# Choosing matmul widths at run time: per expert on three engines, or per group of 12 or 24 products on TensorE alone

## The chip, the core and the metric

One core of one Trainium2 chip runs the whole program. The time is the device time of an execution in microseconds, from runs of the kernel on the chip: before the change a median of 905.44 us over 3 runs (902.94 to 908.5). TensorE (PE) multiplies; VectorE (DVE) and ScalarE (ACT) evict its results and convert; GpSimd (POOL) issues gathers and scatters by index; SyncE (SP) issues most other DMAs. SBUF is the on-chip memory, PSUM the banks that PE writes.

## What is computed

Linear attention with an exponential feature map, then a mixture of 8 experts in which each of 2304 tokens goes to one expert, then a dense block with a maximum over three products:

```python
x = num / den                                # attention, 4 x 8 heads x 576 tokens -> 2304 x 512
expert_idx = np.argmax(logits, axis=1)       # logits: cosine of x and 8 embeddings / tau
for e in range(8):
    mask = expert_idx == e
    h = np.maximum(x[mask] @ w1[e], 0.0)     # 512 -> 1024
    out[mask] = gate_w[mask, None] * (h @ w2[e])   # 1024 -> 512
h = np.maximum(np.maximum(x @ w1, x @ w2), x @ w3) # second block, 512 -> 768, float64 weights
y = h @ w_out                                # 768 -> 512
```

## The kernel before, in words

Every float32 operand of the experts and of the second block is split in two (H, rounded to fp32r, and L, the rest), and each product is three: wH x H, wL x H, wH x L. Weights come by DMA as `raw` tiles of 1 MB, ScalarE rounds them to `wH` and VectorE subtracts for `wL` (`split_w`, L893).

The attention ends near 204 us. The routing then holds, on the chip, how many tokens each expert has, and the list of tokens sorted by expert. GpSimd gathers rows of x in that order, 128 a tile (`gather`, L867); PE transposes a tile into PSUM (`turn`, L874) and ScalarE copies it to the long tile `xy`, whose columns are the sorted tokens.

How many columns an expert's products need is known only at run time. `Routing.sizes` holds 17 widths, 256 to 512 in steps of 16. For expert e, PE, ScalarE and VectorE load the index of the width (`regs`, L934), and `choose` (L967) builds a binary tree of `If`s with 17 leaves; each leaf is `arm` (L981), the whole expert written out at one width:

- 8 times `A` (L898): 12 products of 128 x N into one PSUM bank, ScalarE's relu and VectorE's subtraction into `hx`; `split_w` of the two second-layer tiles after f = 1 and 3; the turning of the tiles that the next expert needs after f >= 1;
- `split_x` (L888) for the next expert's tokens and `split_w` for its first-layer weights (for the last expert: `split_y(0)` and two conversions of second-block weights, `prep_m2`, L1077);
- 4 times `B` (L911): 24 products into one bank, ScalarE's copy to `xy`.

So a tree holds 17 x 192 products in PE's program, 192 of which run. After the eighth expert an `If` (L1235) passes over `redo`, which does experts of more than 512 tokens in pieces; it isn't taken here.

The second block (`second`, L1110) goes over token groups g of 512, 256, 512, 512 and 512 columns and six slices f of the hidden 768. `S1(g, f)` is 36 products in three banks: ScalarE copies the first bank to `m2m` (L1134), VectorE takes the maximum with the other two (L1136), ScalarE rounds (`hH`, L1138) and VectorE subtracts (`hL`). `S2(g, f)` multiplies that with `w_out`. The weights are float64: `prep_m2` makes float32 H and L of one half slice out of the two 32-bit halves, one operation of ScalarE (L1086), three of VectorE (L1087 to L1089), one of ScalarE (L1090) and one of VectorE (L1091). During g = 0 and 1 a conversion stands ahead of each S1:

```python
for f in range(NF):
    for g in (0, 1):
        n = 2 * f + 2 + g
        self.prep_m2(n)
        self.load_m2(n + 2)
        S1(g, f, (6, 7))
        if f:
            S2(1 - g, f - 1, ...)
```

All order is written by hand: each engine runs its instructions in program order and waits for semaphores.

Of the kernel before, what the change touches and what calls it, by code (L numbers as in the profile page):

```python
# [601 lines left out]
class Routing:  # L602


    STEP, MIN, CAP = 16, 256, 512

    def __init__(self, tc, gp, rp, NT, E):
        self.tc, self.nc, self.gp, self.rp = tc, tc.nc, gp, rp
        self.NT, self.E = NT, E
        self.sizes = list(range(self.MIN, self.CAP + 1, self.STEP))  # L610

    def prep(self, n):
# [28 lines left out]
        self.th = iota(rp, [1, len(self.sizes) - 1], [[self.STEP, len(self.sizes) - 1]], "th", base=self.MIN)  # L641
# [41 lines left out]
    def blocks(self, bank, wbank):  # L683
# [32 lines left out]
        nv = len(self.sizes) - 1  # L716
# [116 lines left out]
class Mlps:  # L833


    S = 256
# [27 lines left out]
    def row(self, nm, dt=F32):  # L864
        return self.pool.tile([128, 512], dt, tag="xs", name=nm, bufs=6)
# [8 lines left out]
    def turn(self, d):  # L874
        ps = self.bank()
# [22 lines left out]
    def A(self, N, f, slots=(0, 1)):  # L898
        nc, P = self.nc, 128
        xH, xL = self.xe  # L900
        ps = self.bank()
        for k in range(4):
            i = slots[k // 2]
            c = (k % 2) * 1024 + f * P
            for q, (w, x) in enumerate(((self.wH, xH), (self.wL, xH), (self.wH, xL))):
                nc.tensor.matmul(ps[:, 0:N], w[i][:, c:c + P], x[:, k, 0:N], start=(k == 0 and q == 0), stop=(k == 3 and q == 2))  # L906
        hH, hL = (h[f // 4][:, f % 4, 0:N] for h in self.hx)
        nc.scalar.activation(hH, ps[:, 0:N], AF.Relu)  # L908
        nc.vector.scalar_tensor_tensor(hL, ps[:, 0:N], 0.0, hH.bitcast(F32), op0=ALU.max, op1=ALU.subtract)  # L909

    def B(self, N, d, o, slots=(2, 3)):  # L911
# [3 lines left out]
        for f in range(8):  # L915
            i, c = slots[f // 4], (f % 4) * 512 + d * P
            for q, (w, h) in enumerate(((self.wH, hH), (self.wL, hH), (self.wH, hL))):
                nc.tensor.matmul(ps[:, 0:N], w[i][:, c:c + P], h[f // 4][:, f % 4, 0:N], start=(f == 0 and q == 0), stop=(f == 7 and q == 2))  # L918
        nc.scalar.copy(self.xy[:, d, bass.ds(o, N)], ps[:, 0:N])

    def experts(self, between):

        tc, nc, rt, ex, E, NT, S = self.tc, self.nc, self.rt, self.ex, self.E, self.NT, self.S
        ET = mybir.EngineType
        sizes = rt.sizes
# [7 lines left out]

        def regs(e):  # L934
# [142 lines left out]
    def prep_m2(self, n):  # L1077
        if n >= 12:
            return
# [188 lines left out]
```

## Time and profile before

| | us |
|---|---|
| median of 3 runs | 905.44 |
| the profiled execution, as timed | 905.33 |
| its span, first to last instruction | 903.6 |
| PE busy | 754.9 (84%) |
| VectorE busy | 392.5 (43%) |
| ScalarE busy | 336.2 (37%) |
| GpSimd busy | 139.9 (15%) |

The attention runs to about 204 us, the experts from 227 to 548, the second block from 560 to 888; the last scatters end the span. A row of the timeline gives the start, the duration, engine, line, operation and in brackets the idle time of the engine just before, with what ended it. Products are pipelined: a product's duration is longer than the distance to the next one. A branch isn't counted as busy; its records stand under the sequencer of an engine (PEldq is PE's).

### The profile page before, as it was taken

What the parts mean: (1) busy time and instruction counts of PE and PEld (TensorE: products, weight loads), DVE (VectorE), ACT (ScalarE), POOL (GpSimd) and SP (SyncE); (2) the same over time, 40 slices, a digit from 0 to 9 for tenths busy, and PEclk for the clock granted to TensorE, in tenths of its full rate; (3) what the DMA queues carried; (4) which work ended last, traced back from release to release, by engine and by line L of the source; (5) the groups of instructions that cost most, each with busy time, mean ns of one, the idle gap of its engine ahead of it and who ended that gap; (6) DMA issues with size and microseconds to landing.
All of it is one profiled execution on the core that took longest, in us unless ns stands there. A gap on an engine that the chain in (4) does not pass through costs nothing. (4 is left out here: it accounts for less than half of the span.)

```text
span 903.6 us, 13141 instructions
## 1 busy us (share of the span) xinstructions
PE 754.9 (84%) x5459; PEld 626.9 (69%) x5459; DVE 392.5 (43%) x591; ACT 336.2 (37%) x576; POOL 139.9 (15%) x111
## 2 busy tenths in 40 slices
PE   8899999991944998919596984788889999999993
PEld 6665666551944888919596984677778888888882
DVE  7966766773430524605151644655532212111210
ACT  4867576753521534605151542322212212112111
POOL 2733243405400100043000000000000201100001
PEclk9999999995886999959887996999899999999997
DMA  9715332246430425423222503332100100000001
GB/s 199 166 48 128 93 79 83 71 154 211 133 131 12 132 95 189 143 54 95 98 94 99 178 13 99 116 118 93 47 1 12 59 0 12 36 1 23 24 1 46
DMA packets 59795, 76.48 MB, mean 85 GB/s; under 512 B 11632, under 2 KB 41976, under 8 KB 59648
## 3 DMA queue, kind: packets, MB, share of 16 engines
q1 hardware_dynamic: 55712, 64.53, 23.6%
q0 software_dynamic: 3456, 9.46, 3.0%
q8 instruction: 83, 1.36, 0.7%
q14 instruction: 64, 0.52, 0.2%
q10 hardware_dynamic: 480, 0.61, 0.2%
HBM read 65.12 MB, written 9.46 MB: 83 GB/s over the span
## 5 line engine op out<-in xcount | busy, mean ns | idle before, releaser
L906 PE MATMUL b<-xeH,wH 128*128 128x256 f32 (+4 forms) x256 | 88.5, 346 | 69.9 <-issue 69.2
L1136 DVE TENSOR_TENSOR m2m<-m2m,b 128x512 f32<-128x512 f32 (+1 forms) x60 | 38.0, 634 | 164.5 <-PE b L1132 164.3
L906 PEld LDWEIGHTS b<-xeH,wH 128*128 128x128 f32 x256 | 54.4, 212 | 73.6 <-issue 71.1
L909 DVE SCALAR_TENSOR_TENSOR hxL<-b,hxH 128x256 fp32r<-128x256 f32 (+4 forms) x64 | 30.1, 492 | 165.5 <-ACT hxH L908 139.9
L1153 POOL DMA_INDIRECT out_dram<-raw,c2t x18 | 21.2, 1180 | 459.3 <-DVE m2h L1139 280.2
L906 PE MATMUL b<-xeH,wL 128*128 128x256 f32 (+4 forms) x256 | 86.0, 336 | 0.0
L906 PE MATMUL b<-xeL,wH 128*128 128x256 f32 (+4 forms) x256 | 85.6, 334 | 0.0
L341 POOL PARTITION_ALL_REDUCE mq<-pq x32 | 69.3, 2215 | 95.4 <-ACT pq L339 89.3
L896 DVE TENSOR_TENSOR wL<-raw,wH 128x2048 fp32r<-128x2048 f32 x32 | 72.6, 2289 | 18.1 <-ACT wH L895 16.8
L918 PE MATMUL b<-hxH,wH 128*128 128x256 f32 (+4 forms) x256 | 79.6, 311 | 0.0
L918 PE MATMUL b<-hxL,wH 128*128 128x256 f32 (+4 forms) x256 | 79.5, 311 | 0.0
L918 PE MATMUL b<-hxH,wL 128*128 128x256 f32 (+4 forms) x256 | 79.4, 310 | 0.0
L908 ACT ACTIVATE hxH<-b 128x256 fp32r<-128x256 f32 (+4 forms) x64 | 28.4, 447 | 136.8 <-PE b L906 112.3
L1138 ACT CAST m2h<-m2m 128x512 fp32r<-128x512 f32 (+1 forms) x30 | 17.4, 579 | 147.6 <-DVE m2m L1136 147.6
L1132 PE MATMUL b<-xeH,wH 128*128 128x512 f32 x144 | 57.5, 399 | 12.9 <-ACTq L1235 12.0
L895 ACT CAST wH<-raw 128x2048 fp32r<-128x2048 f32 x32 | 60.1, 1901 | 0.7 <-DVE bi L728 0.7
L1132 PE MATMUL b<-xeH,wL 128*128 128x512 f32 x144 | 57.0, 396 | 0.0
L1132 PE MATMUL b<-xeL,wH 128*128 128x512 f32 x144 | 56.9, 395 | 0.0
L906 PEld LDWEIGHTS b<-xeL,wH 128*128 128x128 f32 x256 | 54.2, 212 | 1.9 <-DVE xeL L886 0.2
L906 PEld LDWEIGHTS b<-xeH,wL 128*128 128x128 f32 x256 | 54.4, 212 | 1.4
L1149 PE MATMUL b<-wH,m2h 128*128 128x512 f32 x144 | 51.0, 414 | 0.0
L918 PEld LDWEIGHTS b<-hxH,wH 128*128 128x128 f32 x256 | 48.5, 189 | 1.4
(227 smaller groups left out, 1612.2 us busy)
## 6 DMA issues: line engine op xcount, KB each, us to landing
raw<-in_moe_w_dram SPq DMA_DIRECT2D x32, 1024.0 KB, 5.1
raw<-in_moe_w_dram SPq DMA_DIRECT2D x18, 512.0 KB, 3.7
q<-in_q_dram SPq DMA_DIRECT2D x8, 576.0 KB
kv<-in_v_dram SPq DMA_DIRECT2D x8, 512.0 KB, 6.6
x_d<-x SPq DMA_DIRECT2D x16, 256.0 KB, 2.1
kv<-in_k_dram SPq DMA_DIRECT2D x7, 512.0 KB, 6.1
raw<-in_moe_w_out_dram SPq DMA_DIRECT2D x6, 512.0 KB, 4.5
kv<-in_k_dram SPq DMA_DIRECT2D x2, 256.0 KB
```

The lines of the kernel that those rows point to most:

```text
L341: nc.gpsimd.partition_all_reduce(mx.rearrange("p a b -> p (a b)"), d.rearrange("p a b -> p (a b)"), P, ReduceOp.absmax)
L895: self.nc.scalar.copy(self.wH[i], r)
L896: self.nc.vector.tensor_tensor(self.wL[i], r, self.wH[i].bitcast(F32), op=ALU.subtract)
L906: nc.tensor.matmul(ps[:, 0:N], w[i][:, c:c + P], x[:, k, 0:N], start=(k == 0 and q == 0), stop=(k == 3 and q == 2))
L908: nc.scalar.activation(hH, ps[:, 0:N], AF.Relu)
L909: nc.vector.scalar_tensor_tensor(hL, ps[:, 0:N], 0.0, hH.bitcast(F32), op0=ALU.max, op1=ALU.subtract)
L918: nc.tensor.matmul(ps[:, 0:N], w[i][:, c:c + P], h[f // 4][:, f % 4, 0:N], start=(f == 0 and q == 0), stop=(f == 7 and q == 2))
L1132: nc.tensor.matmul(b, w[:, c], y[k], start=(k == 0 and q == 0), stop=(k == 3 and q == 2))
L1136: nc.vector.tensor_tensor(m, m, b, op=ALU.max)
L1138: nc.scalar.copy(hH, m)
L1149: nc.tensor.matmul(ps[banks[c]], h[:, cs], w, start=(f == 0 and q == 0), stop=(f == NF - 1 and q == 2))
L1153: nc.gpsimd.indirect_dma_start(out=self.out, out_offset=bass.IndirectOffsetOnAxis(ap=rt.c2t[:, t:t + 1], axis=0), in_=o, in_offset=None)
```

## The change

Four widths (256, 320, 448, 512) take the place of 17. The index is loaded on PE alone, except for the very first group. Each A and each B builds its own tree of four bodies on PE (`pick`); the evictions stand behind the tree, once, on all 512 columns. 16 products on whole banks come first, on PE. Gathers are issued tile by tile as their four buffers (six before) come free, and the loads of the next weights stand right behind the split that frees a tile. The last expert does three conversions of second-block weights instead of two. In the second block a conversion is taken apart: `rebias` (ScalarE) for the next piece and `cut` (VectorE, three operations in one buffer, two buffers by turns) for this piece stand ahead of the products of S1, `high` and `low` behind its maxima; S2 of the last slice stands ahead of S1.

```diff
-    STEP, MIN, CAP = 16, 256, 512
+    WIDTHS, CAP = (256, 320, 448, 512), 512
...
-    S = 256
+    S = 512
...
-        return self.pool.tile([128, 512], dt, tag="xs", name=nm, bufs=6)
+        return self.pool.tile([128, 512], dt, tag="xs", name=nm, bufs=4)
...
+    def pick(self, idx, unit, lo=0, hi=None):
+        W = self.rt.WIDTHS
+        hi = len(W) if hi is None else hi
+        if hi - lo == 1:
+            return unit(W[lo])
+        m = (lo + hi) // 2
+        with self.tc.If(idx < m) as c:
+            self.pick(idx, unit, lo, m)
+        with c.Else():
+            self.pick(idx, unit, m, hi)
...
+        self.pick(idx, unit) if idx is not None else unit(512)
+        hH, hL = (h[f // 4][:, f % 4] for h in self.hx)
+        nc.scalar.activation(hH, ps, AF.Relu)
+        nc.vector.scalar_tensor_tensor(hL, ps, 0.0, hH.bitcast(F32), op0=ALU.max, op1=ALU.subtract)
...
+        nxt, idx0 = regs(0), index(0, ET.PE, ET.Activation, ET.DVE)
+        for i in range(16):
+            nc.tensor.matmul(self.ps[i % 8], self.wH[0][:, 0:128], self.wH[0][:, 0:512], start=True, stop=True)
...
+            for f in range(8):
+                if f == 1 and e == 0:
+                    for t in todo:
+                        self.gather(t)
+                self.A(idx0 if first else idx, f, first=first)
+                first = []
+                if f in (1, 3):
+                    self.split_w(2 + f // 2)
+                    if e + 1 < E:
+                        ex.load(2 + f // 2, e + 1)
+                if f >= 4 and todo:
+                    t = todo.pop(0)
+                    keep(t, self.turn(self.xs.pop(t)))
+                    if t + 4 < NT:
+                        self.gather(t + 4)
+            if e + 1 < E:
+                self.split_x(self.xy[:, :, bass.ds(nxt[1] + S, 512)])
+                for i in range(2):
+                    self.split_w(i)
+                    if e + 2 < E:
+                        ex.load(i, e + 2)
+                    else:
+                        self.load_m2(i)
             else:
...
+                self.split_y(0)
+                self.m2_job(3)
             between(e)
...
+            for d in range(4):
+                self.B(idx, d, off)
...
+        def cut():
+            V.tensor_scalar(t, t, 3, None, op0=ALU.logical_shift_left)
+            V.scalar_tensor_tensor(t, lo, 29, t, op0=ALU.logical_shift_right, op1=ALU.bitwise_or)
+            V.scalar_tensor_tensor(t, hi, -0x80000000, t, op0=ALU.bitwise_and, op1=ALU.bitwise_or)
+            self.load_m2(n + 2)
...
+            now, then = prep
+            if then:
+                then[0]()
+            if now:
+                now[1]()
             for i in range(3):
...
+            hH, hL = hT(g, f)
+            if now:
+                now[2]()
             nc.scalar.copy(hH, m)
+            if now:
+                now[3]()
             nc.vector.tensor_tensor(hL, m, hH.bitcast(F32), op=ALU.subtract)
...
         for f in range(NF):
             for g in (0, 1):
...
+                if f:
+                    S2(g, f - 1, b2[g])
+                S1(g, f, (6, 7), (parts.get(n), parts.get(n + 1)))
+                n += 1
```

On PE, where one A of an expert ends and the next begins, before the change (`b` is the PSUM bank, `xeH` and `xeL` the tokens, `wH` and `wL` the weights):

```order
L906 MATMUL b_2878<-xeL,wH_2860 128x256
L906 MATMUL b_2878<-xeH,wH_2860 128x256
L906 MATMUL b_2878<-xeH,wL_2864 128x256
L906 MATMUL b_2878<-xeL,wH_2860 128x256
L906 MATMUL b_2879<-xeH,wH_2859 128x256
L906 MATMUL b_2879<-xeH,wL_2863 128x256
L906 MATMUL b_2879<-xeL,wH_2859 128x256
```

And after the change, the end of the fourth body of one A and the beginning of the next A's tree:

```order
L923 MATMUL b_2881<-xeH,wH_2862 128x512
L923 MATMUL b_2881<-xeH,wL_2866 128x512
L923 MATMUL b_2881<-xeL,wH_2862 128x512
L905 UNCONDITIONAL_BRANCH
L905 COMPARE_AND_BRANCH x2
L923 MATMUL b_2882<-xeH,wH_2861 128x256
L923 MATMUL b_2882<-xeH,wL_2865 128x256
L923 MATMUL b_2882<-xeL,wH_2861 128x256
```

Between two banks stand now a branch and two compares, and three bodies that aren't run. PE's whole program has 10979 rows instead of 30813.

On ScalarE, the beginning of the second block before the change (`raw` under L1086 is the conversion's buffer, `m2m` the running maximum, `m2h` its rounded copy, `y1H` the second group's tokens):

```order
L1105 CAST y1H_38355<-xy 128x512
L1105 CAST y1H_38357<-xy 128x512
L1086 ACTIVATE raw_2509<-raw_2276 128x1024
L1090 CAST wH_2860<-raw_2509 128x1024
L1134 COPY m2m<-b_2880 128x512
L1138 CAST m2h<-m2m 128x512
L1086 ACTIVATE raw_2509<-raw_2505 128x1024
L1090 CAST wH_2860<-raw_2509 128x1024
L1134 COPY m2m<-b_2881 128x256
```

And after it (the running maximum is a part of `xy` now):

```order
L1129 CAST y1H_13298<-xy 128x512
L1093 ACTIVATE raw_2511<-raw_2507 128x1024
L1093 ACTIVATE raw_2511<-raw_2278 128x1024
L1167 COPY xy<-b_2882 128x512
L1102 CAST wH_2862<-raw_2511 128x1024
L1173 CAST m2h<-xy 128x512
L1093 ACTIVATE raw_2511<-raw_2507 128x1024
L1167 COPY xy<-b_2883 128x256
L1102 CAST wH_2863<-raw_2511 128x1024
```

The copy of the first bank has moved ahead of the rounding of the weights (L1090, now L1102), which waits for three operations of VectorE.

On ScalarE, the end of the last expert, before:

```order
L1105 CAST xeH<-xy 128x2048
L1086 ACTIVATE raw_2509<-raw_2276 128x1024
L1090 CAST wH_2859<-raw_2509 128x1024
L1086 ACTIVATE raw_2509<-raw_2505 128x1024
L1090 CAST wH_2859<-raw_2509 128x1024
L919 ISA
L919 COPY xy<-b_2880 128x256
```

and after:

```order
L1093 ACTIVATE raw_2511<-raw_2278 128x1024
L905 UNCONDITIONAL_BRANCH x4
L1102 CAST wH_2861<-raw_2511 128x1024
L1093 ACTIVATE raw_2511<-raw_2507 128x1024
L1102 CAST wH_2861<-raw_2511 128x1024
L1093 ACTIVATE raw_2511<-raw_2278 128x1024
L1102 CAST wH_2862<-raw_2511 128x1024
L945 ISA
L945 COPY xy<-b_2882 128x512
```

A third conversion stands ahead of the evictions of the last B (L919, now L945).

## Rows read from the trace of the kernel before

**Rows 1.** The page: the span, and part 1, busy time of PE.
```profile
span 903.6 us, 13141 instructions
...
PE 754.9 (84%) x5459; PEld 626.9 (69%) x5459; DVE 392.5 (43%) x591; ACT 336.2 (37%) x576; POOL 139.9 (15%) x111
```
**Rows 2.** Waits of PE, 205 to 575 us: total, times, longest.
```profile
PE b L906 <- issue: 69.2, 7, 23.6
PE b L1132 <- ACTq L1235: 12.0, 1, 12.0
```
**Rows 3.** Line L975, branches on PE's sequencer, ns min/median/max; stretches: engines' busy us, clock, DMA.
```profile
L975 PEldq COMPARE_BRANCH  x4: 65/65/78, 329.6 to 330.0; - x4
...
L975 PEldq COMPARE_BRANCH  x1: 3567/3567/3567, 325.5 to 325.5; - x1
...
L975 PEldq COMPARE_BRANCH  x1: 4869/4869/4869, 352.9 to 352.9; - x1
...
L975 PEldq COMPARE_BRANCH  x1: 6723/6723/6723, 515.6 to 515.6; - x1
...
325.53:329.10 3.57, 3.57 (x18) 3.00 (x17) 0.00 (x0) 0.00 (x0) 0.00 (x0) 1.00 0.02 5
352.86:357.73 4.87, 2.30 (x20) 2.10 (x18) 0.29 (x1) 0.37 (x1) 0.00 (x0) 1.00 0.93 363
```
**Rows 4.** Stretches, three of eight experts: busy us, clock, DMA share, GB/s.
```profile
227.00:259.00 32.00, 31.63 (x212) 31.16 (x212) 17.96 (x26) 16.90 (x25) 9.22 (x6) 0.91 0.51 177
...
330.00:358.50 28.50, 25.02 (x208) 24.82 (x208) 14.83 (x15) 15.38 (x22) 0.00 (x0) 1.00 0.43 149
...
523.00:548.00 25.00, 24.70 (x192) 24.50 (x192) 15.42 (x17) 11.40 (x14) 0.00 (x0) 0.93 0.14 44
```
**Rows 5.** Second block: waits of PE, 560 to 700 us; the stretch to 668.
```profile
PE b L1132 <- ACT m2m L1134: 16.6, 6, 4.2
...
580.50:668.00 87.50, 75.14 (x360) 64.17 (x360) 48.68 (x58) 24.57 (x33) 0.00 (x0) 0.90 0.22 72
```
**Rows 6.** Straight code, 664 to 867 us: the stretch; PE's instruction queue (packets, MB, share).
```profile
664.00:867.00 203.00, 203.00 (x898) 166.50 (x898) 43.99 (x59) 35.88 (x55) 17.35 (x14) 0.99 0.05 19
...
q8 instruction: 8, 0.13, 0.3%
```
**Rows 7.** Timeline of PE, 32 products apart; one S1 on the chain that ended last.
```profile
241.01 0.30 PE L906 MATMUL b<-xeH,wH 128*128 128x304 f32 x1
...
245.42 0.30 PE L906 MATMUL b<-xeL,wH 128*128 128x304 f32 x1
...
685.00 8.19 PE b L1132 x36
```
**Rows 8.** Start of the experts: third gather, landing of gathers, first product.
```profile
211.09 1.89 POOL L871 DMA_INDIRECT xs<-x_d,s2t  x1 [0.30 <-issue]
...
DMA to landing us min/median/max: 6.3/6.9/7.5
...
227.32 0.62 PE L906 MATMUL b<-xeH,wH 128*128 128x304 f32 x1 [0.68 <-ACT xeH L885]
```
**Rows 9.** Timeline of ScalarE around the joint to the second block.
```profile
544.16 1.05 ACT L1090 CAST wH<-raw 128x1024 fp32r<-128x1024 f32 x1 [4.44 <-DVE raw L1089]
...
549.82 1.04 ACT L1090 CAST wH<-raw 128x1024 fp32r<-128x1024 f32 x1 [3.55 <-DVE raw L1089]
...
560.40 1.14 ACT L1105 CAST y1H<-xy 128x512 fp32r<-128x512 f32 x2 [8.45 <-ACTq L1235]
...
566.85 0.58 ACT L1134 COPY m2m<-b 128x512 f32<-128x512 f32 x1
```
**Rows 10.** Timeline of PE at a short wait; the stretch around it.
```profile
587.23 0.50 PE L1132 MATMUL b<-xeH,wH 128*128 128x512 f32 x1 [0.91 <-ACT m2m L1134]
...
583.00:597.00 14.00, 10.56 (x57) 8.73 (x55) 8.90 (x10) 4.24 (x6) 0.00 (x0) 1.00 0.29 93
```

More of the change, by code (lines that the diff above doesn't have):

```diff
@@ new lines, in experts, with bring @@
+            todo = [t for t in range(4 * (e + 1), 4 * (e + 2)) if t < NT]
+            first = []
+            if e == 0:
+                for t in (2, 3):
+                    def bring(t=t, ps=self.bank(), d=self.xs.pop(t)):
+                        v = self.turn(d, ps)
+                        self.direct(v, t)
+                        keep(t, v)
+                    first.append((t, bring))
+            for f in range(8):
+                if f == 1 and e == 0:
+                    for t in todo:
+                        self.gather(t)
+                self.A(idx0 if first else idx, f, first=first)
+                first = []
+                if f in (1, 3):
[7 more added lines that the diff above has]
+                        self.gather(t + 4)
@@ L1045, in redo @@
             for d in range(4):
-                self.B(512, d, at)
+                self.B(None, d, at)
         self.split_y(0)
@@ L1085, in prep_m2, with rebias, high, low @@
         H, L = self.WH[f][:, o], self.WL[f][:, o]
[L1086 to L1091 removed]
+        V = nc.vector
+        def rebias():
+            nc.scalar.activation(t.bitcast(F32), hi.bitcast(F32), AF.Copy, scale=REBIAS)
+        def cut():
[3 more added lines that the diff above has]
+            self.load_m2(n + 2)
+        def high():
+            nc.scalar.copy(H, t.bitcast(F32))
+        def low():
+            V.tensor_tensor(L, t.bitcast(F32), H.bitcast(F32), op=ALU.subtract)
+        return rebias, cut, high, low
+    def m2_job(self, k):
+        for _ in range(k):
+            if self.m2n < 12:
+                for p in self.m2_parts(self.m2n):
+                    p()
+                self.m2n += 1
     def split_y(self, g):
@@ L1116, in second, with hT, S1 @@
         hq = self.ew.tile([P, 4, 512], F32R, tag="q", name="m2h", bufs=2)
-        hs = self.row("m2h1", F32R)
-        mm = self.row("m2m")
-        hT = {512: [(hq[:, 2 * i], hq[:, 2 * i + 1]) for i in range(2)], 256: [(hs[:, 0:256], hs[:, 256:512])] * 2}
-        def S1(g, f, banks, prep=None):
+        mm = self.xy[:, 0, self.S + self.NTOK:]
+        def hT(g, f):
+            if g == 1:
+                return hq[:, 2, 0:256], hq[:, 2, 256:512]
+            i = 2 * (f % 2) if g else 0
+            return hq[:, i], hq[:, i + 1]
+        def S1(g, f, banks, prep=(None, None)):
             H, L = self.ys[g]
```

169 lines of the change are left out of this document (49 added, 120 removed).

## The prediction

> **What bounds the kernel now.** I read the page first: the span, and TensorE (PE) busy 84% of it [rows 1]. The question is then what the other 16% are, so the waits of PE come next, for the expert stage alone: 69.2 us before the first product of an expert (L906), in 7 pieces, with "issue" as the releaser, and 12.0 us before the second stage, released by ScalarE's sequencer at the `If` of L1235 [rows 2]. "Issue" means that PE waited for no semaphore that the profile shows. The records of the branch instructions on PE's sequencer say what it did. Four in a row that were not taken stand at 329.6 to 330.0, 65 to 78 ns each and about 0.12 us apart; a branch out of an arm over one further arm took 3.6 us, one over sixteen arms 4.9 us, and one from the third arm to the end of its tree 6.7 us [rows 3]. So a taken branch to a far place costs 3.6 us or more, while PE's instruction queue reads, and one that falls through costs a tenth of a microsecond.
>
> Two more things stand in these rows. While the 4.9 us branch ran, 20 matmuls still started: the sequencer is some 17 to 20 products ahead of PE, about 2 us at 256 columns. And length goes with traffic: 3.6 us at a DMA share of 0.02, 4.9 us at 0.93 [rows 3].
>
> The second cost of a wait is the clock. Each expert stretch shows a granted clock of 0.90 to 0.95 (two of seven shown), the one that starts without a long wait 1.00 [rows 4]: after a far branch PE runs some microseconds at the lower level. Length times (1 - clock) is 32 x 0.09 = 2.9 us in the first and 25 x 0.07 = 1.8 us in the last, 16.6 us over all seven.
>
> The second stage has its own waits: 16.6 us in 6 pieces for ScalarE's first copy of `m2m` (L1134) [rows 5], and a clock of 0.90 over the 87.5 us from 580.5 to 668 [rows 5], thus 8.7 us. After 668 PE never waits: 203.0 us busy of 203 [rows 6].
>
> **The change part by part.** The sum goes against the profiled execution: span 903.6 us [rows 1], 905.33 us as timed, beside a median of 905.44 us. The inputs give 291, 494, 122, 198, 430, 296, 283 and 190 tokens per expert: before 304, 496, 256, 256, 432, 304, 288, 256 columns, after 320, 512, 256, 256, 448, 320, 320, 256.
>
> (a) Far branches between experts go. The trees of 17 arms of 192 products are replaced by trees of four bodies of 12 or 24. No branch then passes more than three bodies. The 69.2 us go, and the 16.6 us of low clock with them: -85.8.
>
> (b) Wider products: 96 columns more over the eight experts, 192 products each. 304 columns come every 0.138 us ((245.42 - 241.01)/32), 512 every 0.227 us (8.19/36) [rows 7], so 0.00043 us per column: 96 x 192 x 0.00043 = +7.9.
>
> (c) Branches inside the experts: 96 groups, each with two compares and one branch out. Not taken, 0.12 us each. A taken branch within a loaded stretch is not in this trace: from below 0.065 us, the shortest record, from above 3.6 to 6.7 us, the far ones. I take 0.2 us, next to the short ones, because target and branch stand at most three bodies apart, and keep the upper end as a rival. At 0.2 us a group costs the sequencer 0.5 us; the 17 products that it is ahead (2 us) cover that. +0.
>
> (d) Reading the code. On the straight stretch from 664 to 867 PE's instruction queue read 8 blocks (0.13 MB, 16 KB each), seven intervals, over 898 products [rows 6]: a block holds 128 products. Now three of four bodies are read and not run. A group of 12 holds 48 products, so a block lasts 128/48 = 2.7 groups, each 12 x 0.117 = 1.4 us at 256 columns (0.138 less 48 x 0.00043): 3.7 us, against 15 us of straight code; 4.6 us at 320 columns, 6.5 at 448 and 7.3 at 512. If the next block is requested when the last is entered, its time must stay below that. The nearest rows are the far branches: 3.6 us with DMA idle, 4.9 to 6.7 us with DMA busy [rows 3]. The weights of an expert keep the DMA share at 0.43 in a 256-column one [rows 4], so a good part of the reads meets traffic. The bounds are 0 (every block in time) and 90 us: 768 products per expert are 6 blocks, 36 in the six experts of 256 or 320 columns, each late by 6.7 - 4.2 = 2.5 us on average. I take +24: half of the 36 late by 1.3 us, since the queued products cover some and idle DMA the rest. The Trainium skill ("Runtime: NRT & Kernel Launch", Instruction fetch mechanics) says that code is read sequentially in 16 KiB blocks, that crossing a block is mostly hidden, and that a branch stalls when its target lies outside the two loaded blocks. The 16 KB and the stalls agree with rows 3 and 6; by its "mostly hidden" this term would be 0 and the sum 24 us lower, by the busy rows it is not.
>
> (e) The start. Tile 2 was ready long before PE came back from two far branches: its gather was issued at 211.09 and such a gather lands 6.9 us later, at 218.0, but the first product stood at 227.32 [rows 8]. Now turn and cast of tile 2 follow the landing, about 1.6 us: first product at 219.6, -7.7. The 16 warm-up products lie in the wait for tiles 0 and 1.
>
> (f) ScalarE and VectorE work on 512 columns always. In a 256-column expert they are busy 15.4 and 14.8 us of 28.5 [rows 4]; 12 evictions of twice the width would have to take over a microsecond more each to reach PE. Their 96 branches, one a group, lead to the next instruction of their own. Gathers now have four buffers instead of six, but each is issued a whole expert ahead, so PE is not late for them. +0; were a tile late, its 6.9 us would show once per expert.
>
> (g) The joint to the second stage. Three conversions instead of two now stand ahead of the last expert's evictions on ScalarE. One takes 549.82 - 544.16 = 5.66 us [rows 9]; so the evictions start 5.7 us later after the last A than before. What goes is one of the two far branches that ScalarE took in the 8.45 us before 560.40, about 4.2 us, and some 3 us of the 6.45 us from there to the first copy of `m2m` at 566.85 [rows 9], which no longer waits for a conversion. The copy thus comes about 1.5 us earlier, some 29 us after the last A, and PE's 12.0 us wait does not vanish: it moves into the first three groups of the second stage, which need that copy to free a bank. Of the next wait, of 4.2 us [rows 5], the pipelined order saves a part: together -4. If the joint gains nothing it costs those 4 us.
>
> (h) The second stage proper. `rebias` of the next piece and `cut` of this one are issued before the products, `high` and `low` behind the copy of `m2m`. That copy no longer stands behind a whole conversion of 5.66 us. From 580.5 to 668 VectorE is busy 48.7 us and PE 75.1 of 87.5 [rows 5], so the conversions fit beside the products once nothing waits for them in turn, and S2 ahead of S1 gives the chain more cover. The other five waits go (16.6 - 4.2 = 12.4), with 8.7 us of low clock: -21.1.
>
> Sum: -85.8 + 7.9 + 24 - 7.7 - 4 - 21.1 = -86.7. From 903.6 that is a span of 816.9; with the 1.7 us around it 818.6, about **819 us**.
>
> **The rivals.**
> 1. Code reading decides: at every block DMA is busy, so (d) reaches its upper end, 90 us. For it: the 4.9 us branch ran under traffic, and the 6.7 us one is longer still, and loads now follow each other sooner. Against: idle gaps remain. 819 + 66 = 885 us, still faster.
> 2. Near branches cost a read like far ones (slower). Each group has one branch out, and the eight experts take 0, 1, 1 or 2 inward (72 in all): 168 taken branches. At 3.6 us, the least of rows 3, these are 605 us of the sequencer's time, of which its 2 us of lead hide at most 192 over 96 groups: 413 us more than without (d), 795 + 413 = some 1210 us. It turns the sign from 1.15 us per group uncovered (110 us over 96). For it: no short taken branch is on record, and even the one over a single arm took 3.6 us. Against: what a far branch waits for is a block that isn't there, and straight code shows no wait at its block borders [rows 6], so the next block is there when it is reached.
> 3. The clock drops from many small gaps (slower too): at the lower of its two levels, half the other, the experts' 240 us of products grow by some 190 us (not all of a product's spacing is the clock's; an estimate): about 1000 us. Rows speak against it: a gap of 0.91 us at 587.23 left the clock at 1.00 [rows 10]. The Trainium skill ("TensorE: Matmul & The Clock Gate", A second HAM failure mode) describes such a kernel, in which short idles between groups of matmuls throttled the clock again and again; the trace has no such case.
> 4. The second stage keeps its waits, because the conversion's loads or VectorE end last: 21 us less gain, 840 us.
>
> **How the numbers follow.** Forecast 0.62, rival 1 0.17, rival 4 0.08, rival 2 0.06, rival 3 0.04, and 0.03 for a mixture that ends within 1% of 905. About 1% is what a measurement of this kernel can tell from no change (its runs spread 0.6%). Faster: 0.62 + 0.17 + 0.08 = 0.87; same 0.03; slower 0.10. The range goes from 790 (nothing late in (d), a little more at the joint) to 880, most of rival 1; what is left out is rivals 2 and 3 and the end of 1.
>
> **What would show it.** Right: no wait of over 2 us before A or B in the waits of PE; branch records of 0.1 to 0.3 us, some of 1 to 3 us at 256 and 320 columns, none at 512; clock 1.00 in the experts; no wait for `m2m` after the first f; instruction blocks at 16 KB, about 50 in the experts. Wrong: branch records of 3 us in every group (rival 2), spacings of 0.25 us (rival 3), waits in the 512-column expert as well (rival 1), or a joint longer than 45 us from the last A to the end of the second group.

## The result and the profile after

The changed kernel takes 806.69 us, the median of 4 runs (804.78 to 813.77); the kernel before took 904.95 us on the same chip (4 runs, 902.94 to 908.5). The ratio is 0.8925, with a 95% interval from 0.8862 to 0.8987. The forecast was 819 us in a range from 790 to 880. The profiled execution of the changed kernel is the longest of the four, 813.77 us; that matters below.

The page of the kernel after, its span and part 1, against [rows 1]. PE runs the same products, a little wider, and 16 more at the start. Its busy time falls by 4.1 us only, the span by 92.1 us: what went is mostly waiting (148.7 us in which PE wasn't busy before, 60.7 us after).

```profile
span 811.5 us, 13326 instructions
...
PE 750.8 (93%) x5475; PEld 620.5 (76%) x5475; DVE 403.0 (50%) x591; ACT 351.8 (43%) x576; POOL 140.5 (17%) x113
```

Waits of PE in the kernel after, 205 to 575 us (total, times, longest), against [rows 2]:

```profile
PE b L1165 <- ACTq L1269: 13.0, 1, 13.0
PE b L923 <- issue: 5.0, 2, 2.7
...
PE b L942 <- issue: 0.8, 3, 0.4
```

The 69.2 us of "issue" ahead of the first A have become 5.8 us, in five pieces ahead of A and B. The wait at the `If` in front of the second stage is still there, 13.0 us instead of 12.0.

Branch records of the kernel after, ns min/median/max, 205 to 480 us, against [rows 3]:

```profile
L905 PEldq COMPARE_BRANCH  x276: 65/176/4341, 219.4 to 476.2; - x138
```

By the trace's records 120 of the 276 last at most 0.09 us (branches not taken), 121 last 0.1 to 0.3 us, 24 last 0.3 to 1 us and 11 longer; the branches between arms took 3.6 to 6.7 us. The longest, 4.34 us, begins at 326.1, inside an expert of 256 columns.

Stretches of the kernel after (busy us of PE, PEld, DVE, ACT, POOL, then clock, DMA share, GB/s), against [rows 4] for the third and fourth expert (256 columns both) and [rows 5] for 87.5 us of the second stage from its third S1 on.

```profile
300.60:325.30 24.70, 24.70 (x209) 24.70 (x208) 16.77 (x15) 17.49 (x22) 3.01 (x2) 1.00 0.44 148
325.40:354.50 29.10, 26.22 (x201) 25.44 (x201) 17.29 (x16) 16.98 (x20) 0.00 (x0) 0.94 0.46 159
...
512.00:599.50 87.50, 87.50 (x469) 75.48 (x468) 48.04 (x61) 27.54 (x39) 1.99 (x2) 1.00 0.21 73
```

Read the third and fourth experts together: same width, same work, 24.70 us at clock 1.00 and 29.10 us at 0.94. The difference is mostly one late block of code. The trace keeps the start and the duration of every packet of PE's instruction queue, 16 KB each: one ran from 328.07 to 329.06 us, and the branch that began at 326.10 ended at 330.44, 1.38 us after it. All 11 records of over 1 us end 1.4 to 1.5 us after such a packet has landed. The second stage's beginning, which had 75.1 us of PE in 87.5 us at clock 0.90, is now without a gap at 1.00.

Where the time went is read from five points of PE's timeline. Of the kernel before (start, duration, engine, line): the first gather of the stage (POOL), the last product of the experts, the first product behind the first two S1 (it belongs to the third S1), the last product.

```profile
206.57 1.30 POOL L871 DMA_INDIRECT xs<-x_d,s2t  x1 [27.48 <-issue]
...
547.70 0.28 PE L918 MATMUL b<-hxL,wH 128*128 128x256 f32 x1
...
580.23 0.63 PE L1132 MATMUL b<-xeH,wH 128*128 128x512 f32 x1
...
887.52 0.39 PE L1149 MATMUL b<-hxH,m2h 128*128 128x512 f32 x1
```

And of the kernel after, with the first product of the experts, which before stood at 227.32 [rows 8]. The first product behind the first two S1 belongs to an S2 here (L1186), since S2 now stands ahead of the third S1:

```profile
209.99 1.30 POOL L872 DMA_INDIRECT xs<-x_d,s2t  x1 [27.33 <-issue]
...
223.06 0.64 PE L923 MATMUL b<-xeH,wH 128*128 128x320 f32 x1 [0.67 <-ACT xeH L886]
...
478.26 0.28 PE L942 MATMUL b<-hxL,wH 128*128 128x256 f32 x1
...
509.11 0.39 PE L1186 MATMUL b<-wH,m2h 128*128 128x512 f32 x1
...
795.40 0.39 PE L1186 MATMUL b<-hxH,m2h 128*128 128x512 f32 x1
```

| stretch | before | after | difference | predicted |
|---|---|---|---|---|
| up to the first gather (not changed) | 206.57 | 209.99 | +3.4 | 0 |
| to the first product of A | 20.75 | 13.07 | -7.7 | -7.7 |
| experts | 320.38 | 255.20 | -65.2 | -53.9 |
| to the end of the first two S1 | 32.53 | 30.85 | -1.7 | -4 |
| second stage from there | 307.29 | 286.29 | -21.0 | -21.1 |
| tail | 16.1 | 16.1 | 0 | 0 |
| span | 903.6 | 811.5 | -92.1 | -86.7 |

### The profile page after: what moved, and what is told of

It reads as the page before. It is cut to its first block, busy times and chain, and to the rows that moved or that the text cites. A ratio compares the mean times of both kernels' runs of the same rounds, so it can differ in the third digit from the quotient of the medians.

```text
span 811.5 us, 13326 instructions
## 1 busy us (share of the span) xinstructions
PE 750.8 (93%) x5475; PEld 620.5 (76%) x5475; DVE 403.0 (50%) x591; ACT 351.8 (43%) x576; POOL 140.5 (17%) x113
## 5 line engine op out<-in xcount | busy, mean ns | idle before, releaser
L1169 DVE TENSOR_TENSOR xy<-xy,b 128x512 f32<-128x512 f32 (+1 forms) x60 | 38.0, 634 | 173.9 <-PE b L1165 173.4
L923 PE MATMUL b<-xeH,wH 128*128 128x320 f32 (+3 forms) x256 | 84.4, 330 | 3.3 <-issue 2.4
L931 DVE SCALAR_TENSOR_TENSOR hxL<-b,hxH 128x512 fp32r<-128x512 f32 x64 | 42.7, 687 | 87.6 <-ACT hxH L930 85.7
L923 PE MATMUL b<-xeL,wH 128*128 128x320 f32 (+3 forms) x256 | 83.0, 324 | 2.7 <-issue 2.7
L923 PE MATMUL b<-xeH,wL 128*128 128x320 f32 (+3 forms) x256 | 82.9, 324 | 0.0
L942 PE MATMUL b<-hxH,wH 128*128 128x320 f32 (+3 forms) x256 | 81.6, 319 | 0.9 <-issue 0.8
L942 PE MATMUL b<-hxL,wH 128*128 128x320 f32 (+3 forms) x256 | 81.0, 316 | 0.0
L942 PE MATMUL b<-hxH,wL 128*128 128x320 f32 (+3 forms) x256 | 81.0, 316 | 0.0
L1165 PE MATMUL b<-xeH,wH 128*128 128x512 f32 x144 | 57.6, 400 | 13.0 <-ACTq L1269 13.0
L930 ACT ACTIVATE hxH<-b 128x512 fp32r<-128x512 f32 x64 | 38.2, 600 | 58.1 <-PE b L923 57.8
L896 ACT CAST wH<-raw 128x2048 fp32r<-128x2048 f32 x32 | 60.0, 1901 | 0.6 <-DVE bi L729 0.6
L1165 PE MATMUL b<-xeL,wH 128*128 128x512 f32 x144 | 57.5, 399 | 0.7 <-DVEq L1269 0.7
L1165 PE MATMUL b<-xeH,wL 128*128 128x512 f32 x144 | 57.2, 397 | 0.0
L942 PEld LDWEIGHTS b<-hxH,wL 128*128 128x128 f32 x256 | 48.5, 189 | 1.7
```

The source lines that it names most:

```text
L896: self.nc.scalar.copy(self.wH[i], r)
L930: nc.scalar.activation(hH, ps, AF.Relu)
L931: nc.vector.scalar_tensor_tensor(hL, ps, 0.0, hH.bitcast(F32), op0=ALU.max, op1=ALU.subtract)
L1165: nc.tensor.matmul(b, w[:, c], y[k], start=(k == 0 and q == 0), stop=(k == 3 and q == 2))
L1169: nc.vector.tensor_tensor(m, m, b, op=ALU.max)
```

## The experiments

Three groups of runs, each on one chip with its own runs of the kernel before: medians of 903.18 us (the first four below), 900.6 us (S1 ahead of S2, eight widths, one choice for four A, products in the wait) and 901.34 us (the pipelined conversion alone, the kernel before with four widths, three edits at the joint and the changed kernel once more). Where two kernels of different groups are compared, their ratios to the kernel before are. The diffs show the main lines of an edit; `...` stands for the rest.

**No choice at all.** The widths of this input stand in the program.

```diff
-        self.pick(idx, unit) if idx is not None else unit(512)
+        unit(idx or 512)
...
-            idx = index(e, ET.PE)
+            idx = (320, 512, 256, 256, 448, 320, 320, 256)[e]
...
```

> The changed kernel with the widths of this input (320, 512, 256, 256, 448, 320, 320, 256) written into the program: no trees, no branches, no bodies that aren't run. Theory (a near branch is hidden by the products that the sequencer is ahead; only late code blocks show): the two waits of 2.4 to 2.7 us before A and the half clock behind them go, and little else: -5 to -12 us, 795 to 802 us, the 256-column experts still 24 to 25 us. Rival (the 96 choices cost time that no wait shows, 0.2 to 0.5 us each): -20 to -45 us, and every expert gets shorter.

Measured: 800.34 us (799.34 to 804.17), ratio 0.8874 [0.8829, 0.8918], by ratios some 5 us less than the change, with intervals that overlap. The two longest of its waits of PE, 200 to 815 us:

```profile
PE b L1165 <- ACTq L1269: 12.2, 1, 12.2
PE b L971 <- ACT wH L896: 3.4, 1, 3.4
```

No line of them names "issue" any more. The experts take 244.4 us from first product to last B, 10.8 us less than in the profiled execution of the change. All of that lies in three of them, by the first product of each in the timeline (fourth 29.2 to 23.9, fifth 43.3 to 38.9, last 24.0 to 22.9); the other five keep their lengths within 0.1 us. So in five experts out of eight, two compares and a branch every 12 or 24 products cost nothing that shows: the theory, not the rival. PE's instruction queue reads 13 blocks there, 49 with the choice.

**No loads of weights.**

```diff
                 if f in (1, 3):
                     self.split_w(2 + f // 2)
-                    if e + 1 < E:
-                        ex.load(2 + f // 2, e + 1)
...
-                    if e + 2 < E:
-                        ex.load(i, e + 2)
-                    else:
+                    if e + 2 >= E:
                         self.load_m2(i)
```

> The changed kernel without the loads of the experts' weights after the first expert's and the two issued at the very start: all later experts compute with the weights that happen to stand in the buffers (this part of the computation is left out); trees and branches are as in the changed kernel. Theory (a block of code is late only where its reading meets DMA traffic): the waits of 2.4 to 2.7 us in the fourth and fifth expert and the branch record of 4.3 us go, no record in the experts stays over 1.5 us, -5 to -12 us, 795 to 802 us. Rival (a block takes 3.3 us to read in any case, against 3.7 us at 256 columns): waits and records as they are, within 2 us of the changed kernel.

Measured: 801.24 us (798.56 to 801.95), ratio 0.8865 [0.8825, 0.8905]. The stretch of its experts, with the DMA share at 0.11:

```profile
222.50:470.00 247.50, 245.37 (x1596) 233.41 (x1596) 138.89 (x136) 132.65 (x151) 36.30 (x30) 0.99 0.11 30
```

The waits of the fourth and fifth expert are gone, as expected, but one of 1.7 us ahead of an A came up elsewhere, and a branch record of 2.38 us remains where none over 1.5 us was expected. Its five records of over 1 us end 1.3 to 1.4 us after a packet of the instruction queue, as in the change: a branch waits for code with little other traffic too. And the repeat of the changed kernel (below) has only 1.2 us of such waits with all its loads. So this run doesn't settle that DMA traffic makes a block late; it shows that little of the time hangs on it.

**Two early conversions.**

```diff
-                self.m2_job(3)
+                self.m2_job(2)
```

> The changed kernel with two conversions of second-block weights, not three, ahead of the last expert's evictions; the third goes to the pipeline of the second stage. Theory (the joint ends with ScalarE, whose conversions stand ahead of the evictions): the evictions start 5 to 6 us earlier, PE's wait of 13.0 us at the If falls to 7 to 8 us, -4 to -6 us, 801 to 803 us. Rival (the joint ends with the load of the raw weights or with the branches at the If): 0, or +1 to +4 because the pipeline then has one conversion more beside products.

Measured: 798.6 us (792.78 to 801.28), ratio 0.8822 [0.8773, 0.8872]; the wait of PE at the `If` is 6.0 us:

```profile
PE b L1165 <- ACTq L1269: 6.0, 1, 6.0
```

The theory holds: 7.0 us of wait went, one conversion and the 1.88 us for which its raw weights were late (see (g) below). Behind the `If` PE waits 0.7 us in all up to 815 us, so the third conversion costs no wait in the second stage. That edit of the change was a step back: the repeat of the changed kernel has 0.8907 [0.8878, 0.8936].

**Conversions in one piece.**

```diff
-            now, then = prep
-            if then:
-                then[0]()
-            if now:
-                now[1]()
+            now = prep[0]
+            for p in now or ():
+                p()
...
-            if now:
-                now[2]()
             nc.scalar.copy(hH, m)
-            if now:
-                now[3]()
...
-        parts[n][0]()
```

> The changed kernel with each conversion of the second stage run in one piece ahead of its S1, as before the change; the order S2 ahead of S1 and the three early conversions stay. Theory (the pipelining is what took the waits away): waits of PE for the copy of m2m come back, 8 to 15 us, with half clock behind them, +12 to +22 us, 819 to 829 us. Rival (S2 ahead of S1 alone gives the chain its cover): +0 to +4 us, no wait over 1 us behind the first f.

Measured: 824.47 us (820.05 to 826.83), ratio 0.9128 [0.9076, 0.918], 2 points above the change. The waits of PE from 480 to 620 us:

```profile
PE b L1163 <- ACT xy L1165: 12.6, 4, 4.2
PE b L1163 <- ACTq L1262: 12.4, 1, 12.4
```

The waits for the copy of the first bank are back, with the same longest, 4.2 us, as in [rows 5].

**The kernel before with the pipelined conversion alone**, S1 still ahead of S2; the conversion is taken apart into four functions as in the change:

```diff
-                self.prep_m2(n)
-                self.load_m2(n + 2)
-                S1(g, f, (6, 7))
+                S1(g, f, (6, 7), (parts.get(n), parts.get(n + 1)))
...
```

> The kernel before with the conversion taken apart as in the change (rebias of the next piece and cut of this one ahead of S1, high and low behind the maxima, two buffers by turns), in the order of S1 and S2 of before. Theory (taking the conversion apart carries most of the gain; with it undone alone the changed kernel lost 17.8 us): the waits for the copy of m2m go, -12 to -18 us, 885 to 892 us. Rival (only both together help: S1 ahead of S2 leaves the chain without cover): -5 to +2 us, waits for the copy of m2m over 10 us in all.

Measured: 881.47 us (878.51 to 882.68), ratio 0.9765 [0.9725, 0.9804], a gain of 20 us and a little more than expected. Its second stage in the stretch of [rows 5]:

```profile
580.50:668.00 87.50, 86.79 (x466) 74.77 (x465) 50.46 (x62) 27.09 (x37) 0.00 (x0) 1.00 0.21 73
```

Undone alone it costs 18 us (0.9128 against 0.8925), done alone it brings 20. In its profile the stage from the end of the first two S1 to the last product takes 287.1 us, against 307.29 before and 286.29 after the change. So the pipelining carries the second stage's gain, and the order of S1 and S2 adds little.

**S1 ahead of S2 in the changed kernel.**

```diff
-                if f:
-                    S2(g, f - 1, b2[g])
                 S1(g, f, (6, 7), (parts.get(n), parts.get(n + 1)))
                 n += 1
+                if f:
+                    S2(g, f - 1, b2[g])
```

> The changed kernel with S1 of a slice ahead of S2 of the last slice, as before the change (S2 of the same group, though), and the conversions taken apart as in the change. Theory (taking the conversion apart carries most of the second stage's gain, the order the remaining 5 to 6 us of the 23.8): +2 to +8 us, 809 to 815 us, with short waits of PE for the copy of m2m. Rival (without the new order the conversion's chain is as late as before): +15 to +22 us, 822 to 829 us.

Measured: 824.75 us (823.11 to 827.38), ratio 0.9154 [0.9102, 0.9207]. This run tells nothing of its question. In the changed kernel the `m2h` of a group has one buffer in these slices, so that S2 now reads the h of the slice after its own and must wait for that slice's cast. Its waits of PE, 480 to 815 us, name it:

```profile
PE b L1186 <- ACT m2h L1173: 11.9, 10, 1.4
PE b L1186 <- DVE m2h L1176: 2.3, 7, 0.4
```

No run here gives it a second one; the run above answers the question in its place.

**Eight widths.**

```diff
-    WIDTHS, CAP = (256, 320, 448, 512), 512
+    WIDTHS, CAP = (256, 288, 320, 352, 384, 432, 480, 512), 512
```

> The changed kernel with eight widths (256, 288, 320, 352, 384, 432, 480, 512) for each group, so seven of eight bodies are read and not run; for this input 48 columns less than with four widths, which is worth 48 x 192 x 0.00043 = -4 us. A block of 128 products now lasts 1.33 groups of A: 1.9 us at 256 columns, 2.3 us at 320, 3.6 us at 512. Theory (one block is read ahead, in about 3.3 us): the experts of 256 to 320 columns wait for nearly every block, 12 blocks x 3.3 us = 40 us instead of 24 to 28 us, in six experts +60 to +100 us, 870 to 905 us, with branch records of 1 to 4 us throughout; the 512-column expert stays within 2 us. Rival (reading keeps up and a third compare costs a tenth of a microsecond that the queued products hide): -4 to +4 us, 803 to 811 us.

Measured: 921.39 us (915.93 to 933.3), ratio 1.0205 [1.0122, 1.0287]: slower than the kernel before the change. The waits of PE, 205 to 575 us:

```profile
PE b L942 <- issue: 32.0, 14, 4.1
PE b L923 <- issue: 22.9, 15, 3.4
...
PE b L878 <- issue: 7.7, 5, 3.3
```

And three of its experts, of 256, 512 and again 256 columns:

```profile
323.60:366.90 43.30, 31.48 (x209) 29.75 (x208) 17.11 (x15) 18.36 (x22) 1.89 (x2) 0.85 0.33 114
269.50:323.40 53.90, 46.80 (x208) 37.29 (x209) 18.18 (x21) 17.56 (x20) 4.64 (x4) 1.00 0.30 101
553.40:589.40 36.00, 26.34 (x192) 24.74 (x192) 22.87 (x22) 15.87 (x17) 0.00 (x0) 0.95 0.19 63
```

The queue's counts in the first and the last of these stretches (packets, MB, share) are

```profile
q8 instruction: 12, 0.20, 1.7%
...
q8 instruction: 11, 0.18, 2.1%
```

so on average a block every 43.3 / 12 = 3.6 us at a DMA share of 0.33, and every 36.0 / 11 = 3.3 us at 0.19. The starts of the single packets show the pace itself: of the 100 distances between blocks in the eight experts 59 are 2.9 to 3.4 us, the median is 3.2 us. The last expert, of 256 columns, takes as long as its code at this pace, not as its products. With four widths a block lasts 3.7 us at 256 columns, so the change stands just on the safe side of this edge. By the first products of the profiled executions the six narrow experts lost 99 us, the upper end of what was expected; the 512-column expert, expected within 2 us, lost 8.6 us and the fifth 4.9 us, together more than was foretold (115 us by the ratios). Why the widest lost anything, these rows don't tell. One rival isn't separated: a branch out of the first body of a B passes 168 products here, against 72 with four widths, and B has 32.0 us of the waits; the 22.9 us ahead of A, whose branches pass at most 84, speak for the pace.

**One choice for four A.**

```diff
+            for f, ps in zip(fs, pss):
+                for k in range(4):
...
-            for f in range(8):
+            for fs in ((0,), (1, 2, 3), (4, 5, 6, 7)) if e == 0 else ((0, 1, 2, 3), (4, 5, 6, 7)):
...
```

> The changed kernel with one choice for four A (48 products) instead of one for each A (12 products), but for the first A of the first expert; the two conversions of the second half of the weights stand ahead of the group, the evictions behind it; B is as it was. Half as many choices in all, the same code and the same number of blocks, but a branch now passes up to 144 products (18 KB), more than a block. Theory (a branch is cheap where its target lies in the block at hand or in the one read ahead, and costs a read of 3.3 us or more where it lies beyond): out of the first body, in the 256-column experts, twice an expert, 3.3 us or more less 2 us of lead; with low clock behind them and with some waits at the borders of A and B, +15 to +40 us, 820 to 845 us, records of over 3 us in the 256-column experts, which get 3 to 6 us longer. Rival (a choice costs by its number, not by its reach): -3 to +2 us.

Measured: 814.94 us (810.63 to 822.53), ratio 0.9072 [0.9007, 0.9136]. Branch records:

```profile
L905 PEldq COMPARE_BRANCH  x136: 65/178/4565, 228.1 to 475.8; - x136
```

The theory isn't borne out, and not ruled out either. The third expert, of 256 columns, takes 25.4 us from first product to first product, against 24.8, not 3 to 6 us more: its long records, four of 1.5 to 2.1 us, are about as long as the sequencer's lead. The fourth, also of 256 columns, takes 27.5 us and has a record of 3.67 us; in the two profiles of the change it takes 29.25 and 24.05 us, so it doesn't decide. From the first product to the last B the experts take 256.3 us, about as in the change's profiled execution (255.2), but 10 us more than in its repeat (246.2): some 3 us each in the first, at whose end PE waits 2.9 us for a rounding of weights (L896), and in the fourth. The waits with "issue" are 5.1 us in all, no more than the change's 5.8. So the branches over up to 144 products don't show the waits of the arms of 192 products before (next run). By ratios the median lies 13 us above the change, just below the theory's range; the profiled execution, 810.63 us, is the lowest of its four, so where the rest of that comes from is open.

**The kernel before with four widths**, still one choice per expert for three engines:

```diff
-        self.sizes = list(range(self.MIN, self.CAP + 1, self.STEP))
+        self.sizes = [256, 320, 448, 512]
...
```

> The kernel before with four widths (256, 320, 448, 512) instead of 17, still chosen once per expert for PE, ScalarE and VectorE together, arms of 192 products. The wider products cost +7.9 us. Theory (what costs is that an arm of 192 products, 24 KB, is more than is read ahead, so that the branch out of one and into the next always waits for a read): the seven waits ahead of an expert stay, at 3 to 9 us each, 25 to 60 us of PE instead of 69.2, with half clock behind them: 870 to 905 us. Rival (the 17 arms and five levels of compares cost it, not the length of an arm): waits under 10 us in all, 820 to 840 us.

Measured: 870.41 us (868.37 to 872.32), ratio 0.9649 [0.961, 0.9687]. The branch records of PE, and the waits of PE from 205 to 575 us:

```profile
L977 PEldq COMPARE_BRANCH  x23: 65/4057/6692, 216.9 to 515.8; - x23
```

```profile
PE b L908 <- issue: 36.5, 5, 11.9
...
PE b L879 <- issue: 4.5, 1, 4.5
```

Fewer arms bring 31 us of the 98. But half of the branches still take 4.06 us or more, and 41 us of waits stay: the theory, at the lower end of its range. The rest of the experts' gain comes from the small groups and from choosing on PE alone; these two weren't separated.

**Products in the wait at the `If`** (with two early conversions):

```diff
+        b = self.bank()
+        for i in range(24):
+            nc.tensor.matmul(b, self.wH[2][:, 0:128], self.wH[2][:, 0:512], start=True, stop=True)
```

> The run with two early conversions (798.6 us), and 24 products of 512 columns into a bank that nobody reads behind the last B, where PE waits 6.0 us at the If. Theory (the clock falls because PE stands still there: the granted clock from 478 to 512 us was 0.87, 4.4 us of low clock): the products take about 5.5 us of a wait that is there anyway, the clock stays at 1.00 into the second stage, -2 to -5 us against the run with two early conversions, 794 to 797 us. Rival (the clock falls for another reason, or the products delay the If): 0 to +3 us, 798 to 802 us.

Measured: 797.2 us (793.71 to 800.34), ratio 0.8842 [0.8786, 0.8899]. The stretch from 472 to 500 us of this run, and then of the run with two early conversions alone:

```profile
472.00:500.00 28.00, 24.15 (x122) 20.20 (x121) 18.45 (x22) 12.48 (x18) 0.00 (x0) 1.00 0.36 119
```

```profile
472.00:500.00 28.00, 21.29 (x105) 17.58 (x104) 17.37 (x21) 11.59 (x17) 0.00 (x0) 0.82 0.37 122
```

The clock is as the theory has it: it stays at 1.00. But the first S1 starts 8.5 us behind the last product of B, against 6.3 us without these products, so that the two nearly cancel: from the last product of B to the end of the first two S1 it takes 22.4 us, against 22.9. Whether it pays can't be told, since two early conversions alone have 0.8822 with an interval that overlaps.

**Three edits at the joint.**

```diff
+                if e + 1 == E and f == 4:
+                    early = [self.m2_parts(n) for n in range(2)]
+                    for p in early:
+                        p[0]()
...
+                for p in early:
+                    p[1]()
+                for p in early:
+                    p[2]()
+                    p[3]()
+                self.m2n = 2
                 self.split_y(0)
-                self.m2_job(3)
...
+        b = self.bank()
+        for i in range(10):
+            nc.tensor.matmul(b, self.wH[2][:, 0:128], self.wH[2][:, 0:512], start=True, stop=True)
```

> The changed kernel with three edits at the joint: two early conversions instead of three; those two pipelined (both rebias within the last expert's A, then cut, cut, high, low, high, low) and put ahead of the cast of the first group's tokens; 10 products into a bank that nobody reads behind the last B. In the run with 24 such products ScalarE waited 4.42 and 3.35 us for VectorE's cut, and the first S1 stood 8.4 us behind the end of the last B. Theory (the chain of conversions on ScalarE and VectorE is what PE still waits for): the first S1 comes some 3 us behind the last B, the clock stays at 1.00, 4 to 5 us less than with 24 products (797.2 us): 791 to 795 us. Rival (the If's join or the loads of the raw weights end last): 796 to 799 us.

> The changed kernel once more, on the chip and in the rounds of the run with the three edits at the joint, so that the two are compared directly: 803 to 810 us by every theory; the difference is 10 to 15 us if the conversions and the low clock hold the joint, 6 to 9 us if the If's join does.

Measured: 797.51 us (796.29 to 801.08), ratio 0.8845 [0.8817, 0.8874], beside the changed kernel once more at 803.73 us (798.64 to 805.75), ratio 0.8907 [0.8878, 0.8936]. So 6 us less than the change, where the rival forecast lay (796 to 799 us, a difference of 6 to 9), and no more than the single edit to two conversions gives. PE still waits 3.2 us at the `If`, and behind it the clock is 0.58 from 476.8 to 484.0 us; that it stays at 1.00 was expected and did not come. ScalarE's timeline in the run with the three edits shows what holds it:

```profile
468.17 1.05 ACT L1114 CAST wH<-raw 128x1024 fp32r<-128x1024 f32 x1 [2.07 <-DVE raw L1110]
469.12 1.90 ACT L1141 CAST xeH<-xy 128x2048 fp32r<-128x2048 f32 x1
473.44 2.06 ACT L945 COPY xy<-b 128x512 f32 x4 [2.42 <-DVE xeL L1142]
```

The second conversion is done at 469.2, but the evictions into `xy` wait 2.42 us until VectorE has read `xy` for the first group's tokens, which the new order put behind the conversions. The chain of conversions was shortened and the wait moved to what stood behind it. The cast ahead of the pipelined conversions is the order to try next; it wasn't tried.

## Why the prediction was right

**(a), (b), (d) Branches, width and code.** Predicted -85.8 + 7.9 + 24 = -53.9 for the experts, measured -65.2. Far branches and their low clock went as predicted, and the lead of the sequencer hides the near ones: the run without a choice leaves -76.0 for the experts, against -77.9 of (a) and (b). Rival 2 (near branches cost a read, 1210 us) is out by the records, of which 11 of 276 are over 1 us, and by that run; it counted 168 taken branches, and there are 156, since the last of four bodies has none behind it. What was mis-sized is (d). It is 5.8 us of waits and two spells of half clock in this execution. The stretches of the kernel after around them, with both waits (first and third) and the stretches behind them:

```profile
326.10:330.45 4.35, 2.29 (x20) 2.09 (x18) 1.38 (x2) 2.71 (x4) 0.00 (x0) 1.00 0.53 195
330.70:336.00 5.30, 5.25 (x31) 5.26 (x32) 3.11 (x3) 1.47 (x4) 0.00 (x0) 0.68 0.30 67
356.03:359.05 3.02, 0.36 (x2) 0.19 (x1) 0.00 (x0) 0.00 (x0) 0.00 (x0) 1.00 0.59 64
359.05:363.00 3.95, 3.95 (x12) 3.52 (x12) 0.69 (x1) 0.60 (x1) 0.00 (x0) 0.57 0.08 4
```

The second wait lies inside a body: a packet of the instruction queue lands at 357.63, and PE goes on 1.4 us later. With 5.30 x 0.32 + 3.95 x 0.43 = 3.4 us of clock that is 9.2 us, not 24. And it changes from one execution to the next: from first product to last B the experts take 255.2 us here, 246.2 us in the profile of the repeat and 244.4 us with no choice, so 2 to 11 us. Half of 36 blocks were taken as late by 1.3 us; PE waited five times, 2.4 and 2.7 us twice and 0.2 to 0.4 us three times. The estimate's place was right, since blocks of 3.7 us stand against reads of 2.9 to 3.4 us, and the run with eight widths shows what lies beyond the edge. The error was to price a block by the far branches of 4.9 to 6.7 us. The term was a guess between 0 and 90 us, and its size decides how near the forecast came: with 9.2 in place of 24 the sum would be 804 us. The sign of being right that goes with it, no wait of over 2 us before A or B, failed twice. About 50 blocks were foretold in the experts, and the queue's count is

```profile
q8 instruction: 49, 0.80, 1.3%
```

The Trainium skill ("Runtime: NRT & Kernel Launch", Instruction fetch mechanics) calls the crossing of a block mostly hidden; these traces agree for the change, and not for eight widths. Rival 1 (code reading decides, 885 us) is out for this kernel, and is what the eight widths did.

**(c)** was right: five of eight experts have the length of straight code.

**(e) The start.** Predicted -7.7, measured -7.7 from the first gather on. In this execution the gathers themselves came 3.4 us later, in a part that wasn't changed. In the profile of the repeat they stand where they stood before, and the first product where it was foretold (219.6):

```profile
206.85 1.30 POOL L872 DMA_INDIRECT xs<-x_d,s2t  x1 [27.34 <-issue]
...
219.88 0.63 PE L923 MATMUL b<-xeH,wH 128*128 128x320 f32 x1 [0.67 <-ACT xeH L886]
```

**(f)** was right: no wait of the experts names a wide eviction for over 0.3 us, nor a gather after the first two.

**(g) The joint.** Predicted -4, measured -1.7; most of this step failed. ScalarE's timeline after, against [rows 9]:

```profile
479.28 1.04 ACT L1102 CAST wH<-raw 128x1024 fp32r<-128x1024 f32 x1 [3.36 <-DVE raw L1098]
...
482.21 1.12 ACT L1093 ACTIVATE raw<-raw 128x1024 f32<-128x1024 f32 x1 [1.88 <-DMA raw<-in_moe_w_dram]
486.61 1.04 ACT L1102 CAST wH<-raw 128x1024 fp32r<-128x1024 f32 x1 [3.28 <-DVE raw L1098]
487.56 2.04 ACT L945 COPY xy<-b 128x512 f32 x4
491.82 1.14 ACT L1129 CAST y1H<-xy 128x512 fp32r<-128x512 f32 x2 [2.22 <-ACTq L1269]
...
498.12 0.59 ACT L1167 COPY xy<-b 128x512 f32<-128x512 f32 x1 [2.46 <-PE b L1165]
```

The step had PE's 12 us wait move into the first groups of the second stage, and ScalarE's copy come 1.5 us earlier. Instead PE stood at the `If` until ScalarE had come there, behind three conversions and the evictions, so the third conversion was a wait of PE's in full; its raw weights came 1.88 us late on top. The far branches went, and gave more than was foretold: ScalarE's 8.45 us at the `If` became 2.22. But the conversions took that back, and the copy, 6.45 us behind that point before, is 6.3 us behind it now: it waits for the products (L1165) in place of a conversion, and after 13.0 us of standing still these ran near half clock (0.54 from 491 to 500 us). What is left of the gain is the next wait, which the step also named: 4.2 us before, 0.5 us after. Reading the 12.0 us before the change as "released by ScalarE's sequencer" would have told it: whatever stands ahead of ScalarE's arrival at the `If` is PE's. In the run with two conversions 7.0 us of that wait are gone.

**(h) The second stage.** Predicted -21.1, measured -21.0; the pipelining alone gives 20. Rival 4 (its waits stay) is out. Rival 3 (small gaps cost the clock) is out too: between the two late blocks the clock stands at 1.00 from 336 to 356 us, over branches in every group.

## What to carry to other kernels

Code that is read and not run has a price per block: compare how long a block's products last with the pace at which blocks are read (here 2.9 to 3.4 us), and stay on the long side. Four bodies of 12 or 24 products did, eight didn't, and the second came out slower than the kernel that it was to improve. A choice on one engine in small groups is free while that engine's queue has more work in it than the branch takes; where engines meet at an `If`, all that the last of them has queued ahead is paid by the others, so put work behind the meeting, not ahead of it.

## What was not expected

A taken branch over up to 144 products takes 1.5 to 2.1 us in the third expert of the run with one choice for four A, between the 0.2 us of a near branch and the 3.6 us of a far one. That isn't a third price. The record of 2.08 us, from 306.27 to 308.35, has no packet of any queue that starts in it, and the DMA view counts a packet at its start; but a packet of PE's instruction queue ran from 305.84 to 307.00. The branch ended 1.35 us after that, and all 12 records of over 1 us in the experts of that run end 1.3 to 1.5 us after such a packet. So these branches wait for a block as well; the earlier its reading began, the shorter they are.

Late blocks are a matter of the single execution: the same program had 5.8 us of such waits in one profile (the longest of four executions) and 1.2 us in another (the shortest of six), so a price per block from one trace needs a second one beside it.
